# Pacing background matmuls in a four-layer attention kernel: any credit left, or a credit over 0.6, before a tile's next group

## The chip, the cores and the metric

The kernel runs on one core of one Trainium2 chip. The metric is device time in microseconds (us). TensorE is called PE here (its weight loads PEld), VectorE DVE, ScalarE ACT, GpSimd POOL and SyncE SP.

## The reference

Input is x of 2048 positions by 640 features in bfloat16. Four times, x is normalised and an attention with 32 heads of width 20 is added to it. Layers 0 and 2 (weights A) see a window of 256 positions, layers 1 and 3 (weights B) see all positions.

```python
def _B_ref(x, wqkv, wo):
    qkv = (x @ wqkv).reshape(B, S, 3, H, Dh).transpose(2, 0, 3, 1, 4)
    q, k, v = qkv[0], qkv[1], qkv[2]
    scores = jnp.einsum("bhqd,bhkd->bhqk", q, k) * (Dh ** -0.5)
    p = _softmax(scores, axis=-1)          # _A_ref masks the scores first
    o = jnp.einsum("bhqk,bhkd->bhqd", p, v)
    return o.transpose(0, 2, 1, 3).reshape(B, S, D) @ wo

x = A_x
x = x + _A_ref(_layernorm(x), A_wqkv, A_wo)
x = x + _B_ref(_layernorm(x), B_wqkv, B_wo)
x = x + _A_ref(_layernorm(x), A_wqkv, A_wo)
x = x + _B_ref(_layernorm(x), B_wqkv, B_wo)
```

## The kernel before

Positions are cut into 4 chunks of 512, heads into 8 groups of 4. A *unit* is one layer, one chunk of queries and one head group (for layers 1 and 3 on the first chunk, also one part of the keys). The list of units is written out (lines 729 to 748) so that windowed units of one layer stand between full units of the next. A *bank* holds the scores of one head against one block of 128 keys, 128x512; a unit is a row of banks.

The main loop (lines 1259 to 1404) goes over *tiles* of two, three or four banks. Up to the fourth part of layer 1's first chunk, tiles of three and two banks alternate; later most have three. PSUM has eight banks: 0 to 2 and 3 to 6 take the scores of even and odd tiles, 7 collects the product with the values, and 5 and 6 also serve the background work when a tile leaves them free. For each tile the loop issues, in this order:

1. unread matmuls owed from before (line 1292) and the score matmuls (line 1298);
2. the exponential on ACT, scores to `pt` (line 1329);
3. `load_ahead`, then `pump` with the tile's rate as credit (line 1341), then `keep_clock` (line 1342);
4. the products of an earlier tile's `pt` with the values (line 1363);
5. a step of the exponentials that DVE computes by itself (`side_step`), and DVE's multiplication of the last tile's `pt` with the window masks (line 1399).

All other work is *background*: Python generators (tasks) in a list ordered by the unit that needs them, `todo`, and a second list, `tails`. The tasks: `stats` (DVE statistics of x for a chunk of layer 0), `ln` (layer norm: a power on POOL, a scaling on DVE, five transposes per 128 rows on PE, lines 393 to 443), `v` (values, five matmuls 128x320 at line 471 a group), `k`, `q` and, for the first chunk, `qk` (projections, five matmuls 128x512 at line 370 a group), `out` (output projection, eight matmuls at line 558 a group) and `tail` (softmax normalisation of a unit, lines 1030 to 1103). A *group* is the row of matmuls that accumulates in one bank and the copy that empties it; once it is begun ("hold"), it is finished in the same tile. The copy is at `evac`: on ACT (line 318) while the unit is before the first layer-1 unit, which starts at tile 77, and on DVE (line 320) afterwards. Stores of q, k and v to scratch memory and loads of projection weights are issued on POOL; q, k and v of a unit are loaded by SP. A weight tile is loaded two ahead, and its user waits at least four tiles (lines 328 to 357).

`pump` adds the tile's rate to the credit (capped at the rate plus 0.1) and advances tasks while `choose` gives one: a begun group first, then tails whose waiting time is over, then, unless credit is used up, the first task of `todo` that is not waiting. A step costs 0.22 for a matmul of a projection, 0.14 for one of values or output, 0.4 for a transposed block; waits and the step that closes a task cost nothing. The rate is 1.2 before tile 77 and then, up to tile 1199, the largest of 0.66 or 0.33 and what the due times ask for, at most 1.0; from the last layer's second chunk on it is 0.45 (lines 1236 to 1248). `keep_clock` advances further tasks, or issues matmuls that nobody reads (line 640), while the tile's count of PE work is below a bound; it does so up to the same place. `require` (line 287) forces tasks through when a unit is due.

The change is in `pump`; the steps below touch `choose`, `advance`, `keep_clock`, `evac` and the tasks.

Of the kernel before, what the change touches and what calls it, by code (L numbers as in the profile page):

```python
# [49 lines left out]
def kernel(  # L50
# [138 lines left out]
    tails = []  # L189
    state = {"tick": 0, "held": None, "credit": 0.0, "early": True, "act": True, "unit": 0, "heat": 0.0, "carry": 0.0, "least": 0.0, "floor": 0.0, "owed": 0}  # L190
# [35 lines left out]
    def advance(task):  # L226
        state["running"] = task
        try:
            kind, n = next(task.gen)
        except StopIteration:  # L230
            drop(task)
            state["held"] = None
            return 0.0
        state["held"] = task if kind == "hold" else None
        if kind == "wait":
            task.wake = state["tick"] + n
            return 0.0
        task.left -= n
        state["heat"] += n / 0.22 * (0.15 if task in tails else 0.7 if task.name[0] == "ln" else 1.0)
        return n  # L240

    def choose(blocked, limit=1 << 30):
        if state["held"] is not None:
            return state["held"]
        for t in tails:
            if t.wake <= state["tick"]:
                return t
        if not blocked:
            for t in todo:
                if t.wake <= state["tick"] and (t.need <= limit or t.holds):  # L250
                    return t
        return None

    def pump(credit, most):
        state["credit"] = min(state["credit"] + credit, most)
        floor = 0.0
        while True:
            t = choose(state["credit"] <= floor)
            if t is None:
                break  # L260
            state["credit"] -= advance(t)
            if t not in tails:
                floor = 0.6


    mfree = {5: (0, 0), 6: (0, 1)}
# [919 lines left out]
    with tc.manual_schedule():  # L1186
# [69 lines left out]
        t = -1  # L1256
        ended = None
        closed = -2
        while ended is None or t < ended + 8:
# [3 lines left out]
            if t < len(tiles) or banks:  # L1263
# [75 lines left out]
                load_ahead()  # L1339
                r = rate(t)  # L1340
                pump(r, r + 0.1)
                keep_clock()
            else:
                ended = t if ended is None else ended
                pump(2.0, 2.0)

            for n in range(2 if n_b == 0 or t > closed + 1 else 0):
# [59 lines left out]
        while tails or todo:  # L1407
            state["tick"] += 1
            pump(5.0, 5.0)
# [30 lines left out]
```

## Time and profile before

| what | us |
|---|---|
| median of 3 runs | 2297.02 (2295.7 to 2298.88) |
| the profiled execution | 2295.7 |
| its span, first to last instruction | 2293.9 |
| ACT busy | 2172.7 (95%) |
| PE busy | 1981.5 (86%), weight loads 709.1 |
| DVE busy | 1468.5 (64%) |
| exponentials (line 1329) | 2105.8 in 1645 + 22 instructions |
| layer 3 from its second chunk on (tile 1200 on) | 1680 to the end |

Per tile, from the start of its first exponential to that of the next, mean us (number of tiles):

| background groups in the tile | tiles 5-79, 2 banks | 3 banks | tiles 80-319, 2 banks | 3 banks |
|---|---|---|---|---|
| none (tails at most) | 1.44 (7) | 1.31 (6) | 0.91 (43) | 1.34 (69) |
| one of projections (k, q, qk) | 1.92 (15) | 1.90 (11) | 1.19 (32) | 1.55 (20) |
| one of values | 1.46 (9) | 1.63 (11) | 1.19 (19) | 1.42 (17) |
| one of the output | 2.49 (3) | 2.62 (5) | 1.06 (11) | 1.48 (13) |
| one block of a layer norm | 2.19 (1) | 1.86 (1) | 1.41 (8) | 1.38 (8) |
| two or more | 2.70 (3) | 3.33 (3) | - | - |

How to read the profile: busy times of PE are of pipelined matmuls whose ends are modelled. "idle before" an instruction is put down to what ended it. In the table of stages each engine's column is its busy time and, in brackets, its number of instructions; PEclk is the share of the clock that TensorE was granted.

### The profile page before, as it was taken

How to read it: one execution, taken by the hardware profiler on the slowest of the kernel's cores; microseconds unless marked ns; L12 is line 12 of the kernel's file. 1: busy time of each engine (PE TensorE's matmuls, PEld its weight loads, DVE VectorE, ACT ScalarE, POOL GpSimd, SP SyncE). 2: the span in 40 equal slices, each digit the busy share in tenths (PEclk: the TensorE clock that was granted, in tenths of full speed). 3: DMA queues.
4: the chain of work that ended last, by engine and by line, in shares of the span. 5: the costliest groups of instructions: out<-in, count | busy, mean ns of one | idle time of the engine just before them, and what ended most of it. 6: DMA issues, size and time to landing. Idle time of an engine off the chain costs nothing.

```text
span 2293.9 us, 40624 instructions
## 1 busy us (share of the span) xinstructions
PE 1981.5 (86%) x15618; PEld 709.1 (31%) x15772; DVE 1468.5 (64%) x2736; ACT 2172.7 (95%) x1742; POOL 273.2 (12%) x445
## 2 busy tenths in 40 slices
PE   8889999989889888888888898898878888888887
PEld 3343343333233333233332333333222222222222
DVE  6777776436656666656676644452677877777772
ACT  6789899999999999999899999999999999999997
POOL 4323223200200112001220012002000000000000
PEclk9899999999999999999999999999765565556556
DMA  6223233321310223102330133103211111111100
GB/s 192 76 56 113 71 87 94 96 75 39 90 33 14 59 69 105 30 15 56 85 98 24 27 86 107 33 19 94 70 36 30 31 36 36 30 32 45 38 17 14
DMA packets 88809, 135.25 MB, mean 59 GB/s; under 512 B 21126, under 2 KB 64006, under 8 KB 88614
## 3 DMA queue, kind: packets, MB, share of 16 engines
q1 hardware_dynamic: 69398, 79.47, 13.0%
q0 software_dynamic: 19216, 53.17, 7.9%
q8 instruction: 124, 2.03, 0.4%
q14 instruction: 71, 0.58, 0.1%
HBM read 98.90 MB, written 27.79 MB: 55 GB/s over the span
## 4 chain that ended last, share of the span: by engine, by line
ACT 41%; PE 30%; issue 14%; DVE 13%; DMA 1%; POOL 0%; SPq 0%; ACTq 0%; another core or an unknown queue 0%; DVEq 0%; POOLq 0%
ACT pt L1329 40%; PE ps L1298 7%; PE ps L370 6%; PE ps L1363 5%; PE ps L558 4%; PE ps L471 3%; DVE pt L1399 3%; PE ps L640 2%; DVE st L320 1%; DVE on L1079 1%; DVE raw_o L911 1%; DVE oT L863 1%; ACT ka L1329 1%; PE ps L1292 1%; DVE x_sb L567 1%
## 5 line engine op out<-in xcount | busy, mean ns | idle before, releaser
L1329 ACT ACTIVATE pt<-ps 128x1536 bf16<-128x1536 f32 (+2 forms) x1645 | 2105.8, 1473 | 84.0 <-PE ps L1298 71.0
L1298 PE MATMUL ps<-qt,kt 32*128 32x512 bf16 x4008 | 637.5, 451 | 161.1 <-ACT pt L1329 130.2
L1363 PE MATMUL ps<-pt,vt 128*21 128x512 bf16 x3872 | 465.3, 452 | 5.9 <-issue 3.8
L1298 PEld LDWEIGHTS <-kt 32*128 32x128 bf16 x4008 | 182.5, 93 | 582.9 <-issue 562.6
L1399 DVE TENSOR_TENSOR pt<-pt,masks 128x1024 bf16<-128x1024 bf16 (+5 forms) x403 | 239.5, 626 | 120.9 <-ACT pt L1329 119.9
L640 PE MATMUL ps<-masks,ident 128*128 128x512 bf16 x655 | 228.5, 385 | 35.2 <-DVE rT L1063 9.2
L370 PE MATMUL ps<-xnT,wqk 128*128 128x512 bf16 x765 | 209.0, 384 | 19.1 <-issue 3.2
L1363 PEld LDWEIGHTS <-vt 128*21 128x21 bf16 x3960 | 99.7, 90 | 315.7 <-issue 304.8
L320 DVE CAST st<-ps 128x512 bf16<-128x512 f32 x134 | 92.5, 690 | 162.0 <-PE ps L370 157.5
L558 PE MATMUL ps<-wop,on 128*128 128x320 bf16 x904 | 161.0, 315 | 8.5 <-DVE x_sb L567 4.0
L1298 PE MATMUL ps<-qa,ka 32*128 32x384 bf16 (+2 forms) x1408 | 118.1, 278 | 27.9 <-ACT pt L1329 22.9
L911 DVE TENSOR_SCALAR xnT<-ps 128x512 int32<-128x512 f32 x88 | 60.8, 691 | 109.0 <-PE ps L904 108.8
L1079 DVE TENSOR_TENSOR on<-oT,ps 128x512 bf16<-128x512 bf16 x128 | 87.5, 683 | 55.5 <-PE ps L1072 51.8
L567 DVE TENSOR_TENSOR x_sb<-x_sb,ps 128x320 bf16<-128x320 bf16 x120 | 58.0, 483 | 95.8 <-PE ps L558 95.4
L471 PE MATMUL ps<-wv,xnT 128*128 128x320 bf16 x640 | 109.2, 300 | 8.4 <-DVE va L320 1.8
L863 DVE CAST oT<-ps 128x512 bf16<-128x512 f32 x112 | 76.8, 686 | 57.1 <-PE ps L1363 38.1
L558 PEld LDWEIGHTS <-on 128*128 128x128 bf16 x904 | 81.5, 101 | 74.7 <-issue 46.6
L370 PEld LDWEIGHTS <-wqk 128*128 128x128 bf16 x830 | 70.3, 97 | 109.0 <-issue 51.2
L640 PEld LDWEIGHTS <-ident 128*128 128x128 bf16 x743 | 57.9, 96 | 128.0 <-issue 126.2
L404 POOL TENSOR_SCALAR rstd<-mv 128x4 f32<-128x4 f32 x15 | 5.4, 363 | 740.7 <-DVE mv L391 738.7
L1363 PE MATMUL ps<-pt,va 128*21 128x384 bf16 (+2 forms) x1408 | 77.7, 282 | 4.2 <-DVE pt L1399 2.4
L1298 PEld LDWEIGHTS <-ka 32*128 32x128 bf16 x1408 | 43.2, 92 | 98.0 <-issue 89.4
(109 smaller groups left out, 1820.2 us busy)
## 6 DMA issues: line engine op xcount, KB each, us to landing
vt<-v_d SPq DMA_DIRECT2D x48, 336.0 KB
kt<-k_d SPq DMA_DIRECT2D x192, 80.0 KB
wqk<-in_B_wqkv_dram POOLq DMA_DIRECT2D x80, 160.0 KB, 3.6
wqk<-in_A_wqkv_dram POOLq DMA_DIRECT2D x70, 160.0 KB, 3.5
k_d<-st POOLq DMA_DIRECT2D x75, 128.0 KB, 2.3
q_d<-st POOLq DMA_DIRECT2D x75, 128.0 KB, 2.2
qt<-q_d SPq DMA_DIRECT2D x384, 20.0 KB
v_d<-vs POOLq DMA_DIRECT2D x16, 336.0 KB, 3.0
```

The lines of the kernel that those rows point to most:

```text
L320: nc.vector.tensor_copy(out=out_, in_=in_)
L370: nc.tensor.matmul(pq, lhsT=wt[:, dc, :], rhs=xt[:, dc, :], start=(dc == 0), stop=(dc == KD - 1),)
L471: nc.tensor.matmul(pv, lhsT=xt[:, dc, i * P : (i + 1) * P], rhs=wv_sb[l % 2][:, dc, h * HD : (h + 1) * HD], start=(dc == 0), stop=(dc == K ...
L558: nc.tensor.matmul(yp, lhsT=on[:, g, qb * P : (qb + 1) * P], rhs=wop[:, g, i * HD : (i + 1) * HD], start=(g == a), stop=(g == b - 1),)
L640: nc.tensor.matmul(ps[:, b, :], lhsT=ident[:], rhs=masks[:, 0, :], start=True, stop=True)
L863: nc.vector.tensor_copy(out=oT[:], in_=op)
L911: V.tensor_scalar(out=xi.bitcast(I32)[:, i * C : (i + 1) * C], in0=side["psum"], scalar1=SCALE * LOG2E * E23, scalar2=127.0 * E23, op0=ALU ...
L1079: nc.vector.tensor_tensor(out=nu, in0=oT[:], in1=zb, op=ALU.mult)
L1298: nc.tensor.matmul(sp[:, i, col * P : (col + qn) * P], lhsT=u.k(kc, j), rhs=u.q(j, q0, qn), start=True, stop=True,)
L1329: nc.scalar.activation(out=pt[:, i:k, b0 * P :], in_=sp[:, i:k, b0 * P :], func=ACT.Exp, scale=SCALE,)
L1363: nc.tensor.matmul(op[32 * j : 32 * j + VW, q0 * P : (q0 + qn) * P], lhsT=u.v(kc, j), rhs=pg[:, i, col * P : (col + qn) * P], start=(first ...
L1399: nc.vector.tensor_tensor(out=pt_[:, i:k, b0 * P :], in0=pt_[:, i:k, b0 * P :], in1=mv_, op=ALU.mult,)
```

## The change

In `pump` the variable `floor` goes, and with it the two lines that raise it to 0.6 once a task outside `tails` has been advanced. The test is then the same at every step: a credit over zero.

```diff
     def pump(credit, most):
         state["credit"] = min(state["credit"] + credit, most)
-        floor = 0.0
         while True:
-            t = choose(state["credit"] <= floor)
+            t = choose(state["credit"] <= 0.0)
             if t is None:
                 break
             state["credit"] -= advance(t)
-            if t not in tails:
-                floor = 0.6
```

`choose`, which takes the outcome of the test as `blocked`, is as before.

## The prediction

> **What bounds the kernel now.** I read the run by stages first, with busy time and granted clock in each. I cut the stages at starts of exponentials on ACT, since each tile issues its exponentials after its scores. Tile 5 starts at 28.7 us, tile 20 at 54.7, tile 40 at 89.0, tile 80 at 170.1, tile 260 at 395.6 and tile 320 at 470.7.
>
> ```profile
> core 0: us, PE busy (x) PEld busy (x) DVE busy (x) ACT busy (x) POOL busy (x), PEclk, DMA share, GB/s
> ...
> 54.70:89.00 34.30, 31.70 (x287) 14.72 (x290) 22.84 (x59) 29.56 (x50) 11.64 (x20) 1.00 0.28 80
> 89.00:111.90 22.90, 16.26 (x136) 6.22 (x135) 17.72 (x47) 12.40 (x11) 5.84 (x8) 0.63 0.25 70
> 111.90:170.10 58.20, 51.70 (x539) 24.99 (x546) 44.82 (x107) 47.50 (x54) 10.31 (x18) 1.00 0.18 51
> 170.10:230.30 60.20, 57.82 (x546) 23.46 (x550) 44.88 (x97) 57.97 (x50) 20.31 (x29) 1.00 0.39 111
> ...
> 470.70:1605.80 1135.10, 991.83 (x8243) 375.68 (x8346) 654.63 (x1268) 1097.26 (x845) 135.99 (x209) 1.00 0.22 58
> ```
>
> There are three regimes. Up to 170 us PE leads (31.70 of 34.30, 51.70 of 58.20) and ACT has gaps. After it ACT is nearly full (57.97 of 60.20) and PE close behind. Between them, 89 to 112 us, every engine is underused and the clock averages 0.63.
>
> Next, what ACT waits for, up to 170 us and then from 170 to 396 us:
>
> ```profile
> ACT pt L1329 <- PE ps L1298: 14.6, 17, 4.4
> ACT ka L318 <- PE ps L370: 4.5, 5, 2.5
> ```
>
> ```profile
> ACT pt L1329 <- PE ps L1298: 13.7, 30, 1.4
> ```
>
> Both times the exponential waits for score matmuls, which stand on PE behind background work issued in the tile before. So a tile with background work is longer than ACT needs, and the position of that work is what the change alters.
>
> Last, the weak stretch in slices of 3 us:
>
> ```profile
> 86.00:89.00 3.00, 2.95 (x33) 1.08 (x33) 1.82 (x7) 2.48 (x5) 2.22 (x3) 1.00 0.71 200
> ...
> 95.00:98.00 3.00, 1.77 (x11) 0.33 (x7) 2.93 (x8) 1.73 (x2) 1.22 (x3) 0.50 0.00 0
> 98.00:101.00 3.00, 2.06 (x19) 0.69 (x19) 2.90 (x9) 1.31 (x1) 2.63 (x4) 0.50 0.32 74
> ...
> 104.00:107.00 3.00, 0.94 (x4) 0.55 (x4) 2.49 (x8) 0.57 (x1) 0.00 (x0) 0.50 0.00 0
> ```
>
> Here DVE is full (2.93, 2.90), PE starves and its clock is at half. In tiles 42 to 47 the background list has nothing to give: the statistics of the next chunks run on DVE, and their layer norm waits for them.
>
> **The change, part by part.** Nothing is removed from the mathematics: exponentials, projections, transposes and DMAs are the same in number. By the two built programs, PE gets 76 more unread matmuls (line 640: 743 to 819; the trace shows 655 of the 743), 2 fewer at line 1292, and 10 projection evacuations go from DVE (line 320) to ACT (line 318). The rest is order.
>
> *The rule.* Before, once anything of the list has advanced in a tile, the next step needs a credit over 0.6. A step that only closes a finished task, or only waits, counts too. After, any credit over zero buys another group. With 1.2 credit a tile before tile 77, the list is spent sooner. Following the planner of both kernels tile by tile: tiles 5 to 79 hold 77 background groups instead of 68 (8 more of projections of queries or keys, 1 more of values), tiles with two or more go from 6 to 16. Tiles 80 to 319 hold 120 instead of 128, and 127 of them hold none instead of 112. From tile 320 to 1199 a few groups change places, and the layer-3 stage has the same work.
>
> *Price in tiles 5 to 79 (141.4 us).* From the starts of the exponentials: tiles without a group last 1.38 us on average, with one projection group 1.91, with one value group 1.55, with two or more 2.7 (two-bank tiles) and 3.3 (three-bank). Three sums:
> - Low end: each extra projection group turns an empty tile into one with a group, 8 x 0.53 = 4.2, and the value group 0.2: +4.4 us.
> - By PE alone: a projection group is 5 matmuls, 1.25 us in the timeline, a value group 0.85: 8 x 1.25 + 0.85 = +10.9 us.
> - By classes: the changed kernel's tiles at the mean of their class are 29 with one projection group (55.4), 16 with two or more (10 x 2.70 + 6 x 3.33 = 47.0), 16 empty (22.0), 6 output (15.3), 7 values (10.9), 1 layer norm (2.2), in all 152.8 us: +11.4 us.
>
> A straight-line fit of the tile times, summed over five tiles, on their banks, groups by kind, layer-norm blocks, tail steps and further unread matmuls gives +5.9. I take +8, between fit and classes, since the doubled tiles are the new ones, and in them the second group cannot hide. The ten evacuations (0.59 us on ACT) fall in this stage, where ACT has 29.56 of 34.30; they are inside these tile means. If they were not hidden, they would add up to 5.9 us.
>
> *Price in tiles 80 to 319 (300.6 us).* An empty tile lasts 0.91 (two banks) or 1.34 us (three), that is ACT alone; with one projection group 1.19 and 1.55, one value group 1.19 and 1.42, one output group 1.06 and 1.48. At these means the changed order is 127 empty tiles (145.7), 45 with one projection group (62.6), 34 values (44.4), 24 output (29.6), 3 layer norm (4.2) and 7 doubled ones at an empty tile plus two groups' excess (11.2), in all 297.7: -3 us. By another route: the stage lasts 27.6 us more than all its tiles empty would (113 x 0.91 + 127 x 1.34 = 273.0), 0.216 for each of 128 groups, and eight of them leave: -1.7. The low bound is -7: tiles 130 to 159 last 43.4 us (230.3 to 273.7) where the fifty before them make 36.1 per thirty, because a due time raises the rate there up to 1.0; with the lead, the rate stays at 0.66, and that crowding may go. The high bound, +1.5, is from the same kind of fit, which puts a price on unread matmuls. I take -3.
>
> *The unread matmuls.* They fill tiles that have no group. The trace has such tiles with and without them: 0.90 against 0.92 us and 1.33 against 1.34. ACT's exponential (1.45 us for 128x1536) hides them: 0. Without that cover it would be 76 x 0.385 = 29 us at the recorded length; no row supports it.
>
> *Rule against row.* In tiles 170 to 230 us PE is busy 57.82 of 60.20 and its weight loads only 23.46. [...]
>
> *DMA and queues.* POOL's weight loads and stores to scratch keep their count and come earlier with their groups. The chain has two waits on such loads, 3.79 us at 283 and 4.49 at 377. New places can remove or add one: -4 to +4, taken as 0, since the loads stay four tiles ahead by the same rule.
>
> *Sum.* +8 - 3 = +5 us on the profiled execution (2295.7 us, span 2293.9 and 1.8 around it): 2300.7. The median shown is 1.3 above that execution, so **2302 us**, +0.22%. With all low terms +4.4 - 7 = -2.6, with all high ones +11.4 + 1.5 = +13; loads widen both by 4.
>
> **Rivals.** Changes within 0.2% (4.6 us) of the median are about what a measurement here cannot tell from none.
> - *A, slower by a little* (2301.7 to 2309): the sum above.
> - *B, nothing*: the order changes but the early groups land where PE would have idled. For it: total work is the same, and the low end of the first term against the second gives +4.4 - 3 = +1.4, 2298.
> - *C, faster*: the lead shortens the half-clock stretch. The list still runs dry for six tiles (now 38 to 43), but the layer norm that follows comes at tile 44, ahead of the output projection, and refills PE in tiles 44 to 47, which before were nearly empty. If full clock came back 15 us earlier, the 10.2 us that PE is busy from 95 to 110 us would be about 5 shorter, and the early groups would stand in what was idle (PE 6.6 us idle from 89 to 111.9), so the first term turns from +8 to -4: -4 - 3 = -7, 2290. Against it: DVE, full from 92 to 104 us, has the same statistics to do. It decides if the dry stretch keeps full clock.
> - *D, slower by much*: doubled groups delay layer norm and tails, a second stretch drops to half clock, and the ten evacuations stand before exponentials: +11.4 + 5.9 - 1.5 = +16, 2313.
>
> On C: the clock fell at 94 us although the longest idle of PE before it was 1.00 us and the matmuls were merely sparse. "TensorE: Matmul & The Clock Gate", Part 1, puts the fall after an idle window of about 3.4 us. By the page neither order loses the clock there and the term is 0; by the trace it is lost with far shorter gaps, and the measurement decides.
>
> **How the numbers follow.** A 0.42, B 0.24, C 0.18, D 0.16. Slower by over 0.2% is A and D, 0.58; within 0.24; faster 0.18. The range goes from 2289, at C's price, to 2315, above D's first 13 us and below its full sum with late loads; it takes in the bounds of the sum and leaves out half of C and a third of D, 0.14.
>
> **What would show it.** In the profile after: tile 80 starts some 8 us later (178 instead of 170.1), tile 320 about 5 later (476), and the distance from there to the end is unchanged within 2 us. ACT's evacuations at line 318 number 79 instead of 69, and ACT's wait for scores before tile 80 grows from 14.6. Wrong would be: tile 80 at or before 170 (C), a stage after 470 us that moves by over 3 us, or a half-clock stretch that the run before does not have (D).

## The result

| | before | after |
|---|---|---|
| runs in turn on one chip, median (us) | 2297.95 (2295.7 to 2300.23, 4 runs) | 2320.91 (2319.01 to 2324.92, 4 runs) |
| the profiled execution, its span | 2295.7, 2293.9 | 2319.01, 2317.2 |
| tile 5 to tile 80 | 141.4 | 146.3 |
| tile 80 to tile 320 | 300.6 | 315.9 |
| tile 320 to the end of the span | 1823.2 | 1826.7 |

The ratio is 1.0102 [1.0085, 1.012]: the changed kernel is 1.0% slower. The direction was forecast, the size was not: 2302 was expected, and 2320.91 lies above the range of 2289 to 2315. Of the 23 us between the two spans, 15.3 arise between tile 80 and tile 320, where a gain of 3 was forecast.

### The profile page after: what moved, and what is told of

It reads as the page before. It is cut to its first block, busy times and chain, and to the rows that moved or that the text cites. A ratio compares the mean times of both kernels' runs of the same rounds, so it can differ in the third digit from the quotient of the medians.

```text
span 2317.2 us, 40790 instructions
## 1 busy us (share of the span) xinstructions
PE 2003.3 (86%) x15686; PEld 719.2 (31%) x15846; DVE 1464.5 (63%) x2726; ACT 2179.1 (94%) x1752; POOL 271.5 (12%) x445
## 3 DMA queue, kind: packets, MB, share of 16 engines
q1 hardware_dynamic: 69398, 79.47, 12.9%
## 4 chain that ended last, share of the span: by engine, by line
ACT 40%; PE 28%; issue 15%; DVE 12%; DMA 0%; POOL 0%; SPq 0%; ACTq 0%; DVEq 0%; POOLq 0%
ACT pt L1326 39%; PE ps L1295 7%; PE ps L367 5%; PE ps L1360 4%; PE ps L555 4%; PE ps L468 3%; DVE pt L1396 2%; PE ps L637 2%; DVE st L317 1%; ACT ka L1326 1%; DVE raw_o L908 1%; DVE on L1076 1%; DVE oT L860 1%; DVE x_sb L564 1%; PE ps L1289 1%
## 5 line engine op out<-in xcount | busy, mean ns | idle before, releaser
L1326 ACT ACTIVATE pt<-ps 128x1536 bf16<-128x1536 f32 (+2 forms) x1644 | 2105.0, 1479 | 97.6 <-PE ps L1295 90.5
L1295 PE MATMUL ps<-qt,kt 32*128 32x512 bf16 x4008 | 638.4, 452 | 163.5 <-ACT pt L1326 133.7
L1360 PE MATMUL ps<-pt,vt 128*21 128x512 bf16 x3868 | 465.5, 453 | 6.3 <-issue 4.3
L1295 PEld LDWEIGHTS <-kt 32*128 32x128 bf16 x4008 | 183.1, 93 | 584.9 <-issue 568.4
L637 PE MATMUL ps<-masks,ident 128*128 128x512 bf16 x723 | 255.8, 390 | 40.1 <-DVE rT L1060 7.1
L1360 PEld LDWEIGHTS <-vt 128*21 128x21 bf16 x3960 | 100.3, 90 | 319.9 <-issue 309.3
L555 PE MATMUL ps<-wop,on 128*128 128x320 bf16 x904 | 158.4, 312 | 7.4 <-DVE x_sb L564 3.0
L1295 PE MATMUL ps<-qa,ka 32*128 32x384 bf16 (+2 forms) x1408 | 117.2, 277 | 27.4 <-ACT pt L1326 22.6
L637 PEld LDWEIGHTS <-ident 128*128 128x128 bf16 x819 | 64.9, 97 | 139.9 <-issue 137.6
L555 PEld LDWEIGHTS <-on 128*128 128x128 bf16 x904 | 80.7, 100 | 71.9 <-issue 44.2
L1360 PE MATMUL ps<-pt,va 128*21 128x384 bf16 (+2 forms) x1408 | 78.8, 281 | 8.7 <-DVE pt L1396 6.3
L1295 PEld LDWEIGHTS <-ka 32*128 32x128 bf16 x1408 | 43.9, 92 | 95.2 <-issue 85.4
```

The costliest lines, as they stand in the source:

```text
L555: nc.tensor.matmul(yp, lhsT=on[:, g, qb * P : (qb + 1) * P], rhs=wop[:, g, i * HD : (i + 1) * HD], start=(g == a), stop=(g == b - 1),)
L637: nc.tensor.matmul(ps[:, b, :], lhsT=ident[:], rhs=masks[:, 0, :], start=True, stop=True)
L1295: nc.tensor.matmul(sp[:, i, col * P : (col + qn) * P], lhsT=u.k(kc, j), rhs=u.q(j, q0, qn), start=True, stop=True,)
L1326: nc.scalar.activation(out=pt[:, i:k, b0 * P :], in_=sp[:, i:k, b0 * P :], func=ACT.Exp, scale=SCALE,)
L1360: nc.tensor.matmul(op[32 * j : 32 * j + VW, q0 * P : (q0 + qn) * P], lhsT=u.v(kc, j), rhs=pg[:, i, col * P : (col + qn) * P], start=(first ...
```

## The profile after

All line numbers behind `pump` are three lower than in the kernel before: the exponential is L1326, the scores L1295, the product with the values L1360. First the stages. The columns are those of the table in the prediction: busy time and number of instructions of each engine, then the clock. Before:

```profile
28.70:170.10 141.40, 122.12 (x1129) 54.36 (x1143) 106.20 (x269) 109.21 (x145) 38.12 (x63) 0.92 0.30 82
170.10:470.70 300.60, 279.91 (x2510) 114.22 (x2537) 200.07 (x423) 282.02 (x240) 85.48 (x128) 1.00 0.33 92
```

The same tiles after:

```profile
28.30:174.60 146.30, 129.76 (x1176) 58.29 (x1192) 105.38 (x264) 114.11 (x155) 50.44 (x81) 0.94 0.35 99
174.60:490.50 315.90, 290.52 (x2517) 117.85 (x2551) 197.32 (x419) 282.01 (x240) 76.08 (x115) 0.98 0.30 81
```

In the second stage ACT does the same work to a hundredth (282.02 and 282.01 us, 240 instructions). DVE and POOL do less, as part of their work went ahead of tile 80. So the 15.3 us are idle time on ACT. What ACT waited for there, in us, times, longest; before and after:

```profile
ACT pt L1329 <- PE ps L1298: 15.2, 34, 1.4
```

```profile
ACT pt L1326 <- PE ps L1295: 33.1, 48, 2.0
```

The exponential waits 17.9 us longer for score matmuls. And PE, in the same stage after:

```profile
PE ps L1295 <- ACT pt L1326: 11.9, 32, 1.0
PE ps L1360 <- DVE pt L1396: 5.3, 10, 1.7
```

The second row is new: its counterpart before (L1363, waiting for L1399) is 0.2 us, once. PE stands in front of the product with the values until DVE has multiplied the masks. Of the 5.3 us, 2.5 stand in tiles that last longer than ACT needs (101, 111 and 189); the other seven waits cost nothing. The largest, and what follows it, is seen at tiles 111 to 113, which last 2.25, 3.42 and 2.28 us (before 0.91, 1.35 and 1.14). The timeline of after there (start, us, engine and line, count, and in brackets the idle time before and its releaser):

```profile
214.97 0.21 DVE L388 BATCH_NORM_AGGREGATE mv<-stats 128x2 f32<-128x12 f32 x1
215.09 1.57 DVE L1396 TENSOR_TENSOR pt<-pt,masks 128x1024 bf16<-128x1024 bf16 x3
...
215.78 0.39 PE L1360 MATMUL ps<-pt,va 128*21 128x256 bf16 x6 [1.67 <-DVE pt L1396]
...
216.78 0.45 DVE L414 TENSOR_SCALAR xn<-x_sb,rstd,nmr 128x640 bf16<-128x640 bf16 x1
...
217.28 0.45 PEld L432 LDWEIGHTS <-xn 128*128 128x128 bf16 x5 [0.74 <-DVE xn L414]
217.28 0.71 PE L432 MATMUL ps<-ident,xn 128*128 128x128 bf16 x5
...
218.22 0.15 PEld L432 LDWEIGHTS <-xn 128*128 128x128 bf16 x1 [0.28 <-DVE xn L414]
...
218.64 0.74 PE L432 MATMUL ps<-ident,xn 128*128 128x128 bf16 x5
...
219.31 0.61 PE L1295 MATMUL ps<-qt,kt 32*128 32x512 bf16 x2
...
219.96 1.02 ACT L1326 ACTIVATE pt<-ps 128x1024 bf16<-128x1024 f32 x1 [1.97 <-PE ps L1295]
...
220.34 0.44 PE L432 MATMUL ps<-ident,xn 128*128 128x128 bf16 x5
```

DVE comes to the masks only after the statistics of a layer norm (the last step is L388). Then two layer-norm blocks (L432, five transposes each) are issued in one tile. Each needs a scaling on DVE (L414), which is queued behind the masks. The next scores (219.31) stand behind both blocks on PE, and ACT is idle for 1.97 us. The clock has a part in this: it is at half speed from 216.6 to 220.0 us, and five transposes take 0.71 and 0.74 us there, 0.44 in the next tile. That tile, 113, holds a pair too, at full clock and with no wait for a scaling, and still lasts 1.37 us longer than ACT needs. Over the whole stage the weight loads of the transposes wait for scalings no longer than before (2.8 us, before 2.9; the rows stand at e9 below). Before, the sixteen blocks of this stage fell one to a tile; after, twelve of them are in six pairs.

A second pattern stands some 14 us earlier, at full clock and with no wait on DVE in the stretch shown:

```profile
201.85 0.39 PE L1295 MATMUL ps<-qt,kt 32*128 32x512 bf16 x3
202.18 1.26 PE L555 MATMUL ps<-wop,on 128*128 128x320 bf16 x8
203.37 0.39 PE L1295 MATMUL ps<-qt,kt 32*128 32x512 bf16 x2
203.69 1.26 PE L555 MATMUL ps<-wop,on 128*128 128x320 bf16 x8
204.88 0.40 PE L1360 MATMUL ps<-pt,vt 128*21 128x512 bf16 x4
205.21 0.39 PE L1295 MATMUL ps<-qt,kt 32*128 32x512 bf16 x3
```

Two output groups (L555) in neighbouring tiles. PE is full from 201.85 on; ACT waits 0.20 us for the first scores and then 0.78 for the next (its exponential at 205.65).

To size both, I took from each tile's length what ACT needs in it (0.91 us with two banks, 1.335 with three) and sorted the rest by what stands in the tile, over tiles 80 to 319:

| excess over ACT's need, us (tiles, mean) | before | after |
|---|---|---|
| projection group | 13.3 (52, 0.26) | 16.7 (45, 0.37) |
| layer norm, one block | 4.4 (16, 0.27) | 0.7 (3) |
| layer norm, two blocks, or one and a group | none | 9.3 (7) |
| output group | 3.6 (24, 0.15) | 9.0 (24, 0.38) |
| values | 6.6 (36, 0.18) | 5.8 (34, 0.17) |
| none | 0.4 (112) | 2.1 (127) |
| sum | 28.3 | 43.6 |

Layer norm makes +5.6, output +5.4, projections +3.4, the rest about +0.9. The six pairs exceed by 1.34 us on average: the two that stand at half clock (tile 112, and tile 193 for half of its length) by 2.13, the other four by 0.95. Position shows in the projection groups: before, 41 of 52 follow an empty tile and exceed by 0.17, 11 follow another group and exceed by 0.56. After it is 25 at 0.13 and 20 at 0.67.

The reason lies, by the code, in how the floor was raised (e4 tries it). A step that only waits, or closes a task, raised it as well. With a waiting task at the head of the list and a rate of 0.66 (credit capped at 0.76), the next group needed a credit over 0.6, which is there in every other tile. Without the floor a credit just over zero starts a group, and after one layer-norm block (0.4) enough is left for a second.

The clock has other low stretches too. In the profiled execution before it is at half speed from 46.3 us for 6.8 us, from 94.1 for 17.1, and from 551.5 and 920.2 for 3.4 each, ahead of layer 3. After, it is from 45.9 (6.8), 93.7 (10.2), and for 3.4 each from 216.6, 247.3, 325.8, 571.6 and 1363.5. The three at 216.6 to 325.8 lie in the stage that lost. 7.0 of its 43.6 us of excess stand in four tiles that they cover in whole or in part: the two pairs named above and two groups of values (tiles 132 and 133). No projection or output group is among them.

## The experiments

The theory: groups in neighbouring tiles and layer-norm blocks in pairs, both after tile 80, make the loss. The rivals: it is the early order (doubled groups, ten more evacuations on ACT); it is the 76 more unread matmuls; it is the half-clock stretches. Each kernel is compared with the kernel before in turn on one chip; stages are of its profiled execution: tiles 5 to 80, tiles 80 to 320, and the rest. Every diff is against the kernel before, unless it says after; lines that only set a new variable up are left out.

**e1 and e2: the change in time.** e1 keeps the floor only before tile 77, e2 only from there.

```diff
-            if t not in tails:
+            if t not in tails and state["unit"] < woven:
                 floor = 0.6
```

```diff
-            if t not in tails:
+            if t not in tails and state["unit"] >= woven:
                 floor = 0.6
```

> The floor of 0.6 is kept while the unit is before the first layer-1 unit (up to tile 76) and dropped afterwards. In tiles 5 to 79 the order is almost that of before (69 groups, 7 doubled tiles), in tiles 80 to 319 it is loose (6 tiles with two or more layer-norm blocks, 45 neighbouring tiles that both hold a group). If the loss is made after tile 80 by the loose order itself: tile 80 starts within 1 us of before's 170.1, the stage of tiles 80 to 319 is 12 to 16 us longer than before's 300.6, and the whole is 2311 to 2318 us. If the loss comes from the lead won in the early tiles: within 5 us of before, 2294 to 2302.

> The mirror image: no floor up to tile 76 (76 groups and 16 doubled tiles in tiles 5 to 79, as in the changed kernel), the floor of 0.6 afterwards (120 groups, none doubled, 27 neighbouring pairs in tiles 80 to 319). If the late order makes the loss: tile 80 starts 4 to 5 us late as in the changed kernel, the stage of tiles 80 to 319 is as long as before's or up to 3 us shorter, and the whole is 2297 to 2304 us. If the lead is the cause: 2310 or more.

Measured: e1 1.0060 [1.0039, 1.0081], stages 142.3, 309.0, 1833.2; its middle stage is 8.4 us longer, not 12 to 16. e2 0.9996 [0.9981, 1.0012], stages 142.9, 295.8, 1836.1; its tile 80 starts 0.4 us late, not 4 to 5. The middle stage of e2, and its wait for scores there:

```profile
170.50:466.30 295.80, 276.51 (x2505) 111.54 (x2502) 194.90 (x417) 280.91 (x241) 75.69 (x114) 1.00 0.31 85
```

```profile
ACT pt L1329 <- PE ps L1298: 10.9, 25, 1.2
```

The early order does no harm by itself. It saves 4.8 us after tile 80, which is the lead that the prediction counted. The loose order after tile 77 loses 8.4 us in the stage without the lead, and 20.1 with it (315.9 against 295.8). So the two do not add: 0.60% and none make 1.02% together. The totals are less clear than the stages: both profiled executions are long behind tile 320 (e1 by 10.0 us, e2 by 12.9). In e2 every tile there holds the same work as before, but its clock is at half for 37.6 us (before 6.8), 13.7 of them from 965.5, and PE waits 2.1 us for one projection weight. Its runs as a whole are not long.

**e3 and e4: which steps raise the floor.** In e3 only layer-norm steps do, in e4 only steps that cost something.

```diff
-            if t not in tails:
+            if t not in tails and t.name[0] == "ln":
                 floor = 0.6
```

```diff
-            state["credit"] -= advance(t)
-            if t not in tails:
+            cost = advance(t)
+            state["credit"] -= cost
+            if t not in tails and cost > 0.0:
                 floor = 0.6
```

> The changed kernel, except that a block of a layer norm raises the floor to 0.6; all other groups are as loose as in the changed kernel (48 neighbouring pairs, 103 unread matmuls in tiles 80 to 319), and no tile from 80 to 319 holds two layer-norm blocks. If pairs of layer-norm blocks, in which PE waits in order for DVE, are the main loss: their tiles lose 8 to 11 us in the changed kernel in that stage, so 2309 to 2314 us. If the spacing of all groups is the loss: 2317 to 2323, as the changed kernel.

> The floor is raised by a step that does work, but not by one that only waits or only closes a task. No tile from 80 to 319 is doubled and none has two layer-norm blocks, but neighbouring tiles that both hold a group go from 36 to 53 (the changed kernel has 41), and unread matmuls there from 62 to 91. If doubled tiles are the loss, this is as before: 2295 to 2301 us. If neighbouring groups are the loss, as slow as the changed kernel: 2310 to 2325.

Measured: e3 1.0099 [1.0067, 1.0131], stages 146.3, 307.3, 1831.7. e4 1.0128 [1.0101, 1.0154], stages 141.1, 329.6, 1832.1. With the pairs undone the stage of e3 is 8.6 shorter than after's, as expected (it has no half-clock stretch there either, so the 8.6 are not all the pairs'), but its total, from 2314 to 2330, cannot be told from after's: inconclusive there. e4 has no doubled tile, and it is at least as slow as after. Its projection groups that follow a group (23) exceed by 0.55, its output groups that follow one (7) by 0.83. Part of its loss is the clock:

```profile
378.00:429.00 51.00, 50.94 (x274) 11.70 (x273) 15.90 (x34) 35.52 (x31) 0.00 (x0) 0.50 0.08 19
```

Half speed for 51 us with PE busy throughout; e4's empty tiles, which cost nothing elsewhere, exceed by 15.8 us together. In the tiles of this stretch stand 18.4 us of excess. Outside them, at full clock, projection and output groups exceed by 26.2 us, before by 16.9. So neighbours cost without any doubling, some 9 of e4's 29 us, and the larger part is the stretch's.

**e5: after, spaced.** From tile 77 a tile that follows one with a projection or output group starts with a floor of 0.6. Against after:

```diff
+        floor = 0.6 if state["last"] == state["tick"] - 1 and state["unit"] >= woven else 0.0
         while True:
-            t = choose(state["credit"] <= 0.0)
+            t = choose(state["credit"] <= floor)
             if t is None:
                 break
-            state["credit"] -= advance(t)
+            cost = advance(t)
+            state["credit"] -= cost
+            if cost > 0.0 and t.name[0] in ("k", "q", "out"):
+                state["last"] = state["tick"]
```

> The changed kernel, with one rule added from tile 77 on: a tile that follows one in which a projection group (q, k) or an output group was issued needs a credit over 0.6 to begin. In tiles 80 to 319, projection and output groups whose tile before held a group too go from 24 to 9 (before: 10); the pairs of layer-norm blocks stay (5 tiles). In the changed kernel such a group makes its tile 0.67 us longer than ACT needs, one after an empty tile 0.13 to 0.30. If spacing is half of the loss: that stage is 5 to 8 us shorter than the changed kernel's 316.0, and the whole 2312 to 2317 us. If spacing costs nothing, 2318 to 2325.

Measured: 1.0031 [1.0018, 1.0044], stages 144.9, 303.9, 1826.8. The stage:

```profile
173.10:477.00 303.90, 281.96 (x2507) 116.06 (x2537) 196.16 (x419) 280.82 (x241) 77.13 (x117) 1.00 0.31 85
```

12.0 of the 15.3 us come back, more than expected, with the layer-norm pairs still there (layer norm exceeds by 10.3 us, after by 10.0) and the clock at 1.00 instead of 0.98. The clock is not the main part of it: the excess of projection and output groups falls from 25.7 to 16.4 us, and after has none of them at half clock in this stage. These 9.3 us are what spacing gives back.

**e13: after, with both undone** (e5's lines, and `if t not in tails and t.name[0] == "ln": floor = 0.6` behind them).

> The changed kernel with both remedies at once and still without the floor for all other steps: a layer-norm block raises the floor to 0.6, and from tile 77 on a tile after a projection or output group begins with a floor of 0.6. If the two costs are separate and add up, tiles 80 to 319 lose both of what they lost singly (8.7 and 12.1 of 316.0 us): 294 to 299 us, and the whole is within 0.3% of before, 2296 to 2304. If they are the same loss counted twice: about 304 there and 2305 to 2309 in all.

Measured: 1.0042 [1.0026, 1.0058], stages 145.5, 302.5, 1827.7. Missed: singly the two bring 8.6 and 12.0, together 13.4. They overlap by 7.2 us. That is about what stands in after's half-clock tiles (7.0), of which e3 and e5 are each rid; that the overlap is the clock's is not shown. What e13 still has over e2, 6.7 us, is mostly projections: their excess is 13.5 against 9.3, with 12 against 7 groups that follow a group.

**e6, e9 and e10: layer-norm pairs alone.** The kernel before, with two blocks to a tile from tile 77 to 306. In e6 both use one PSUM bank (the second `take_m` is left out), in e9 two; e10 is e9 without the unread matmuls ahead of the transposes in these tiles. e9's edit:

```diff
             drop_m(mb)
+            if i % 2 == 0 and woven <= state["unit"] < index[1, 0, 0, PARTS[1][3]]:
+                state["credit"] -= 0.4
+                continue
             yield ("pe", 0.4)
```

> The kernel before, except that in tiles 77 to 306 the blocks of a layer norm are issued two in a tile in the same bank (8 tiles with pairs for the 16 blocks); spacing of all other groups is as in before (10 projection and output groups after a group, 121 groups, 66 unread matmuls). If pairs cost what they seem to in the changed kernel, 1.1 to 1.6 us beyond ACT against 0.27 for a single block: 8 x 1.35 - 4.4 = +6 us, 2302 to 2307 us, with the stage of tiles 80 to 319 at 305 to 309. If they cost nothing: 2296 to 2300.

> As the kernel with layer-norm pairs in one bank, but the second block of a pair takes the other background bank, as the changed kernel's pairs do in this stage, so that its transposes need not wait for the copy of the first. If that wait is what made a pair 3.03 us longer than ACT needs: a pair falls to 1.1 to 1.6 us, tiles 80 to 319 last 303 to 309 instead of 322, and the whole is 2300 to 2309 us. If the pair costs the same in two banks, because PE waits for DVE's scaling: 2318 to 2326.

> The pairs in two banks without the two unread matmuls ahead of each block's transposes in tiles 77 to 306 (the output is not changed by that; unread matmuls there go from 66 to 37). If PE's own work makes the pair long, four unread matmuls of 0.22 us each go from a pair: 0.8 to 0.9 us less for each of 8 pairs, 5 to 8 us less than the pairs with them, unless the clock falls for want of work. If waiting for DVE is the cost, the pair stays as long within 0.3 us.

Measured: e6 1.0115 [1.0082, 1.0147], stages 140.4, 322.2, 1826.4 (305 to 309 expected for the middle one); a pair exceeds by 3.03. e9 1.0053 [1.0037, 1.0069], stages 140.4, 306.9, 1831.4; a pair 1.59. e10 1.0056 [1.0035, 1.0078], stages 140.5, 310.5, 1831.3; a pair 1.6. Weight loads of the transposes waiting for DVE's scaling, in this stage: before, after, e9, e10:

```profile
PEld L435 <- DVE xn L417: 2.9, 2, 1.8
```

```profile
PEld L432 <- DVE xn L414: 2.8, 5, 0.9
```

```profile
PEld L435 <- DVE xn L417: 6.7, 7, 1.8
```

```profile
PEld L435 <- DVE xn L417: 10.6, 13, 2.1
```

Pairs alone make the stage 6.3 us longer in e9 (layer norm exceeds by 12.8 against 4.4, with seven groups fewer in the stage). Its total, +0.53%, is no measure of them: 8.2 us of its profiled execution arise behind tile 320, where the clock is at half for 13.7 us from 973.3. In the stage, too, e9's clock is at half once (from 328.2, 6.8 us): the two pairs there exceed by 2.34 each, the six at full clock by 1.35. In e6 the second block also waits for the first one's copy out of the bank, which after does not do, and 30.7 us of the stage are at half clock (from 236, 256.5 and 338.4 us). Six of its eight pairs stand there; the other two exceed by 1.47, so e6 overstates. e10 does not decide between the wait for DVE and PE's own work. With less work on PE the wait grew, but the clock fell to half three times (from 232 and 253 us for 6.8, from 331 for 10.2) and six of its eight pairs stand there. The two at full clock (tiles 285 and 286) exceed by 0.32, in e9 by 0.72: there PE's own work was part of the price. In e9 6.7 of the 12.8 us of the pairs are waits for DVE; in after's pairs it is 2.4 of 8.1.

**e7: more unread matmuls.** The kernel before, with 56 more in otherwise quiet tiles of the stage:

```diff
                 pump(r, r + 0.1)
+                quiet = state["heat"] < 0.2
                 keep_clock()
+                if quiet and 80 <= t < 320 and spent[0] < 56:
+                    mb = min(mfree, key=mfree.get)
+                    if mfree[mb][0] <= state["tick"]:
+                        spent[0] += 1
+                        nc.tensor.matmul(
+                            ps[:, mb, :], lhsT=ident[:], rhs=masks[:, 0, :], start=True, stop=True
+                        )
```

> The kernel before, with 56 further unread 128x512 matmuls in tiles 80 to 319 that hold no group (the changed kernel has 56 more there than before); nothing else moves. If the unread matmuls are free beside ACT, as tile lengths with and without them say: 2296 to 2301 us, and tiles 80 to 319 last 300 to 302. If they are paid at PE's 0.22 us each: +12 us, 2310.

Measured: 1.0041 [1.0026, 1.0055], stages 140.4, 310.2, 1826.6. Missed: 9.6 us, 0.17 for each. The empty tiles themselves stay as they were (0.01 to 0.02 over ACT's need), but the groups behind them lengthen: projections from 0.17 to 0.29, output from 0.15 to 0.25. In after, the additional ones stand in rows of empty tiles: tiles 215 to 260 last 51.6 us there and 53.6 before. So they are dear ahead of a group, and not what after lost: in e7 41 projection and output groups follow a quiet tile with such matmuls, in after 5 (before 2).

**e12: more warmth early.** `warmth` is 1.76 from the start, which adds four unread matmuls before tile 80 and changes nothing else.

```diff
-                warmth = 1.76 if state["unit"] >= woven else 1.0
+                warmth = 1.76
```

> The kernel before with the bound of PE work per tile, below which unread matmuls are issued, raised from 1.0 to 1.76 for tiles before 77 (4 more unread matmuls there, nothing else moves). If the half-clock stretch at 94 to 111 us is for want of PE work and costs what PE's busy time there suggests, it is shortened and 1 to 5 us are gained: 2292 to 2297. If DVE holds that stretch, the time stays within 0.1%: 2296 to 2300.

Measured: 1.0023 [1.0011, 1.0035], stages 141.5, 300.6, 1830.0. The half-clock stretch at 94 us shrinks from 17.1 to twice 6.8 us, and the stage is not shorter, as it would be if DVE holds it. The loss arises after tile 320, where every instruction is as before (the counts of PE differ from before's only by records that the traces miss):

```profile
470.90:1605.80 1134.90, 1010.99 (x8297) 373.53 (x8295) 652.51 (x1262) 1090.68 (x840) 136.34 (x209) 0.99 0.21 57
```

Half clock falls there at 890 (3.4), 1340.5 (6.8) and 1559 us (6.8), and tiles 860 to 1200 last 482.7 instead of 475.8. Tile by tile, e12 falls behind only at these three places, by 1.4, 2.8 and 4.2 us, and it gains 1.3 us where before has its own stretch at 920. Two of the three begin with a load that comes late for PE:

```profile
1340.52 0.60 PE L1298 MATMUL ps<-qt,kt 32*128 32x512 bf16 x1 [2.07 <-DMA kt<-k_d]
...
1558.38 1.81 PE L370 MATMUL ps<-xnT,wqk 128*128 128x512 bf16 x5 [1.67 <-DMA wqk<-in_B_wqkv_dram]
```

Before, the first of these waits is 0.42 us, followed by one of 0.17, and the second does not occur. So with the same order, late loads and the places where the clock falls move the total by some 0.3%; which of the two moves it more is not separated.

**e8, e11 and e14: looking for a version that gains.** e8 leaves the early order free, keeps the floor and e5's spacing from tile 77, and ends a tile's background work after one layer-norm block. e11 does so with the floor in the early tiles too. e14 is e8 without the rule on layer norm. e8's lines, behind e5's:

```diff
+            if t not in tails:
+                if t.name[0] == "ln" and cost > 0.0:
+                    floor = 9.0
+                elif state["unit"] >= woven:
+                    floor = max(floor, 0.6)
```

> A version built on the two suspected costs: groups are free up to tile 76 as in the changed kernel, but a block of a layer norm ends its tile's background work everywhere; from tile 77 on the floor of 0.6 holds as in before, and also at the start of a tile that follows a projection or output group. Tiles 5 to 79: 70 groups, no pairs of layer-norm blocks; tiles 80 to 319: 126 groups, none doubled, 8 projection or output groups after a group. If pairs and spacing are the causes: tile 320 starts 4 to 8 us earlier than before's 470.7, and the whole is 2290 to 2296 us. If they are not: 2297 to 2305.

> The kernel before with both suspected costs pushed further down everywhere: a layer-norm block ends its tile's background work, the floor of 0.6 holds from the first tile, and from tile 77 on also at the start of a tile after a projection or output group. No tile is doubled at all, but tiles 5 to 79 hold only 63 groups (before 68), tiles 80 to 319 hold 133 (before 128), 14 of the heavy ones after a group (before 10). By the prices found, the early stage gains 5 to 8 us and the later one loses 2 to 4: 2291 to 2296 us; if delay of work matters more than doubling, 2298 to 2305.

> Groups free up to tile 76 as in the changed kernel, from tile 77 on the floor of 0.6 as in before and, further, at the start of a tile after a projection or output group (5 heavy groups after a group in tiles 80 to 319, before 10). If spacing is a cost by itself: tiles 80 to 319 take 293 to 296 us, and the whole is 0 to 0.2% faster than before, 2292 to 2298. If not: as the kernel with the floor from tile 77 on, 2298 to 2301.

Measured: e8 0.9993 [0.9976, 1.0011], stages 141.6, 296.9, 1826.6. e11 1.0039 [1.0026, 1.0052], stages 147.5, 304.7, 1825.5. e14 0.9998 [0.9981, 1.0014], stages 143.0, 296.4, 1833.4. e8 and e14 take the stage 4 us below before (e14 with the lead of after, e8 with two groups of it), but the totals are the same as before's. e11 missed: with early work held back tiles 5 to 79 take 6 us more, with two more half-clock stretches there (128 us for 6.8, 162 for 10.2); the two are not separated. No version beats the kernel before by what can be measured.

## Why the prediction was wrong

- **What bounds the kernel**: right. After tile 80 ACT is full, and what it loses is waiting for scores behind background work.
- **"Price in tiles 80 to 319", -3**: this is the step that failed; it measured +15.3. It took the mean tile of each class and changed the counts. The counts were right, and e2 shows that their gain is real (-4.8). Against its sum of 297.7, projections measured 68.3 for 62.6, output groups 35.1 for 29.6, doubled tiles 16.9 for 11.2 and empty ones 147.4 for 145.7; values and single blocks were as priced. But the means held only for the old spacing, in which four of five projection groups followed an empty tile. The floor had kept the spacing, not only the number per tile. Doubled layer norm was priced like two groups, about 0.5 us; it measured 1.34 a pair, 0.95 at full clock, and e9 shows pairs alone at +6.3 us. Neighbours were not priced at all, and e5 gets 9.3 us back at them by spacing. The three half-clock stretches were not in this price either; up to 7.0 us stand in their tiles.
- **"Price in tiles 5 to 79", +8**: right in sign, mis-sized. It measured +4.9, near the low bound of 4.4. With the same early order e2 and e14 are at 142.9 and 143.0, +1.5, but their clock does not fall at 46 us, while before's and after's both do; so this term is +1.5 to +4.9. The fit of +5.9 was nearer than the class means, which put the six output tiles at 15.3 us (11.4 measured) and the empty ones at 22.0 (19.7).
- **"The unread matmuls", 0**: right for this change and wrong as a rule. The empty tiles were compared by their own length, and e7 shows that the cost falls on the tile behind.
- **DMA, 0 (±4)**: no wait of that size appeared in tiles 80 to 319; PE's one wait for a projection weight there is 1.1 us, before it was 1.0 and 0.3.
- **After tile 320**: under 2 was expected, +3.5 measured, inside what e12 and e2 show with the same order (+6.8 and +12.9 in their profiles).
- **Rivals**: D came nearest in size and was partly right in mechanism (doubled layer norm, new half-clock stretches), but it priced them before tile 80 and blamed the evacuations. Those became more on ACT as foretold, and its wait for scores before tile 80 did not grow (14.1 to 13.4 from tile 5 on). C's mechanism came true, its price did not: the stretch at 94 us is 10.2 us long after and 17.1 before, and tile 80 still starts later; e12 shortens the stretch, too, and nothing is gained.
- **Signs**: tile 80 starts at 174.6 (178 foretold), tile 320 at 490.5 (476).

What stays open: why early lead and loose late order cost more together than singly (20.1 against 8.4 in the stage). The three half-clock stretches that after has there and e1 has not are a part of it. 7.0 us stand in their tiles; at the 1.3 to 1.4 us that a stretch of this length cost at 890 us in e12 and at 920 before, three would make some 4 us (an estimate). Whether the crowding brings the stretches or they come by chance was not tried. How the price of a pair divides between the wait for DVE and PE's own work is open as well.

## What to carry to other kernels

When background work shares an in-order engine with the work that feeds the bottleneck, price where it lands, not only how much there is: an empty tile is not idle, it is the slack from which the neighbour's group is paid. Steps that are chained through another engine cost more in one tile than in two: a pair of layer-norm blocks exceeded by 0.95 us (after) to 1.35 (e9) at full clock, a single block by 0.27. Look at the clock of a stretch before its loss is put down to the order. Compare two versions stage by stage at the starts of the same tiles; a total can hide a gain of 5 us in one stage behind late loads and a clock that falls elsewhere.

## What was not expected of the hardware

- The clock fell to half in stretches of 3.4 us and multiples of it, with PE merely sparse: in the 3.4 us ahead of the fall PE was busy for 1.55 us at 94.1 (before) and for 1.7 to 2.2 us at 216.6, 247.3 and 325.8 (after). Where the bound lies was not tried. After, from 93.7 us, while DVE is full (9.48 of 10.20):

```profile
93.70:103.90 10.20, 8.08 (x53) 3.05 (x54) 9.48 (x26) 4.67 (x5) 2.63 (x3) 0.50 0.13 29
```

- Once at half, it can stay there for 51 us although PE shows no gap (50.94 of 51.00 in e4). What ended that stretch no view shows.
- The Trainium skill, "TensorE: Matmul & The Clock Gate", section A second HAM failure mode: psum-queue depth-cycling, describes a clock that goes back and forth when PE idles briefly and often between groups of matmuls. The falls near 94 us would fit that (PE's longest idle ahead of them is 1.00 us before and 1.84 after); the 51 us in e4 do not.
